# Small VectorE pieces handed out one a step, and a longer slack for the fill of two banks, in a gated mix of two attentions

## The chip, the core and the metric

The kernel runs on one core of one Trainium2 chip. The metric is the device time of one execution in microseconds (us), median of several runs. TensorE (PE) multiplies, VectorE (DVE) and ScalarE (ACT) read its results from PSUM, GpSimd (POOL) works in SBUF, SyncE (SP) only issues DMAs. Each engine works through its own queue in order and waits there for semaphores of the others.

## The reference

The output is a gated sum of two attentions over the same 2048 rows of 512 numbers, all in f32: branch A looks at eight earlier rows at distance 2, branch B is full attention of 32 heads on one shared key and value head.

```python
def _A_ref(x, wqkv, wo):          # H = 32, Dh = 16, W, dil = 8, 2
    ...
    logits = jnp.einsum("bhsd,bhswd->bhsw", q, kg) * scale
    logits = jnp.where(mask[None, None, :, :], logits, -1e9)
    attn = _softmax(logits, axis=-1)
    o = jnp.einsum("bhsw,bhswd->bhsd", attn, vg)
    return (lambda x, *d: x.transpose(*d))(o, 0, 2, 1, 3).reshape(B, S, D) @ wo

def _B_ref(x, wq, wk, wv, wo):    # H = 32, Dh = 16, one key and value head
    ...
    scores = jnp.einsum("bhqd,bkd->bhqk", q, k) * (Dh ** -0.5)
    p = _softmax(scores, axis=-1)
    o = jnp.einsum("bhqk,bkd->bhqd", p, v)
    return (lambda x, *d: x.transpose(*d))(o, 0, 2, 1, 3).reshape(B, S, H * Dh) @ wo

g = _sigmoid((x * gate_w).sum(-1, keepdims=True))
return g * _A_ref(...) + (1 - g) * _B_ref(...)
```

The inputs make the scores of branch B large, so that its softmax needs each row's maximum before the exponential.

## The kernel before, in words

**Units, steps, fills.** Branch B is cut into 32 units, each four heads by 512 queries. A unit takes 16 steps, one for each 128 keys, so the main loop (`for s in range(NS + 1)`, L737) has 512 steps. A step `s` multiplies keys by queries into two PSUM tiles of two banks each (`exp_pair`, L311: two matmuls at L316, then ScalarE's exponential at L318), and adds the weighted values of the step before into the one bank `po` (`weighted`, L323, matmuls at L326). At a unit's end VectorE transposes `po` (`finish_a`, L334, then `finish_b`), GpSimd divides and gates, and after every second unit VectorE transposes the result once more (`finish_c`, L354).

**Maxima.** Before a unit can start, the maximum of each of its 2048 query rows over all 2048 keys must be known. That takes 64 matmuls of 512 columns a unit ("fills", 2048 in all), each followed by a maximum on VectorE. `fill_pair` (L269) fills the two-bank tile `m2` (in the profile pm) with two of them and reduces both in one instruction (L274); `fill_one` (L278) fills the one-bank tile `m1` (in the profile ps) and reduces it (L285). Their matmuls are those of L253. When a unit's last fill is reduced, `filled` (L258) brings the unit's maxima together (two reduces at L264, a transpose at L266); `shift_a` (L289, ScalarE) and `shift_c` (L296, VectorE, L297) split them into two parts, and `shift_b` (L301) writes these by eight small DMAs into the rows of the stacked queries that subtract the maximum within the score matmul.

**The front.** Before the main loop, 78 lumps (14 of query projections, 64 of branch-A projections) are multiplied, with up to four fills after each (`front_fills`, L603, also into `eb[1]` and `po`).

**Branch A** runs on GpSimd in 16 groups. `run_pool` (L655) hands its pieces out when the planner's clock says that GpSimd will soon be free. Three steps of a group are on other engines, with a due time: the maximum (`a_max`, L395, VectorE), the exponential (`a_exp`, ScalarE) and the sum with its reciprocal (`a_sum`, L409, VectorE). Before they stand in a list `hooks`, and `run_pool` calls those that are due.

**Output.** Four times in the main loop `out_phase` (L512) multiplies four blocks of rows by the output weights, with fills between. `out_store` (L494) adds the two halves on GpSimd and stores them.

**What sets the order.** The schedule is written out by hand: the order in which the Python code issues instructions is the order of every queue. A planner decides it with three clocks (`clk` for PE, ACT, DVE) and fixed prices (L42). `after(engine, ready, price)` moves a clock on. `free[bank]` is when the planner believes a bank to be free again. `fill_ready(bank, slack)` (L559) issues a fill if the bank is free no later than `slack` after PE's clock; it then moves PE's clock to that time, so PE is expected to wait for so long. Otherwise the fill is left out of this step. Tasks with a due time are called by `run_tasks` (L598) at a step's end.

In a step of the main loop the order is: exponential pair, `fill_ready("m2")`, the other exponential pair, `fill_ready("m1")` if fills would otherwise not be done in time, `weighted`, `finish_a` at a unit's end, `run_tasks`, `run_pool`. An output phase starts when branch A is through and the fills are less than 1.6 units ahead.

Of the kernel before, what the change touches and what calls it, by code (L numbers as in the profile page):

```python
# [6 lines left out]
F32 = mybir.dt.float32  # L7
F32R = mybir.dt.float32r
AF = mybir.ActivationFunctionType
ALU = mybir.AluOpType  # L10
# [3 lines left out]
P = 128  # L14
# [23 lines left out]
NS = NU * NJ  # L38
NF = 2 * NU * 2 * 4 * 4


T_R, T_LAT, T_EXP, T_RED2, T_RED1, T_W, T_LUMP, T_Q = 0.23, 0.20, 0.92, 1.14, 0.61, 1.18, 2.53, 3.2  # L42


@with_exitstack
def gated_mix_kernel(ctx, tc, xt, wa, wk, wq, wo_a, wo_b, out):
# [33 lines left out]
    def after(eng, ready, dur):  # L80
        clk[eng] = max(clk[eng], ready) + dur
        return clk[eng]
# [168 lines left out]
    def max_mm(dst, v, pr, t, kc, odd):  # L251
        b = 64 * odd
        nc.tensor.matmul(dst, qst[v % NB][b:b + 62, pr, t * P:(t + 1) * P], kst[b:b + 62, kc * 512:(kc + 1) * 512], start=True, stop=True)  # L253

# [3 lines left out]
    def filled(v, n):  # L258
        left[v] -= n
        if not left[v]:  # L260
            ms = wp.tile([P, 2, 2, 8], F32, name="ms")
            m = mx.pop(v).rearrange("p b i t k -> p b (i t) k")
            for x in range(2):
                nc.vector.tensor_reduce(ms[:, :, x, :], m, AX.X, ALU.max)  # L264
            mt = wp.tile([P, 32], F32, name="mt")
            nc.vector.transpose(mt, ms.rearrange("p b x y -> p (b x y)"))  # L266
            tasks.append((after("dve", 0, 0.5) + 0.1, shift_a, (v, mt)))

    def fill_pair(dst, key):  # L269
        v, pr, t, kc = slots.pop(0)  # L270
        m = unit_tile(v)
        for odd in range(2):
            max_mm(dst[:, odd, :], v, pr, t, kc, odd)
        nc.vector.tensor_reduce(m[:, :, pr, t, kc], dst, AX.X, ALU.max)  # L274
        free[key] = after("dve", after("pe", 0, T_R) + T_LAT, T_RED2) + 0.08
        filled(v, 2)

    def fill_one(dst=m1, key="m1"):  # L278
# [5 lines left out]
        max_mm(dst, v, pr, t, kc, odd)  # L284
        nc.vector.tensor_reduce(m[:, odd, pr, t, kc:kc + 1], dst, AX.X, ALU.max)  # L285
        free[key] = after("dve", after("pe", 0, T_R) + T_LAT, T_RED1) + 0.08
# [9 lines left out]
    def shift_c(v, mt, th, ml):  # L296
        nc.vector.scalar_tensor_tensor(ml, mt, mk[:, 5:6], th.bitcast(F32), op0=ALU.mult, op1=ALU.add)  # L297
        after("dve", 0, 0.2)
        shift_b(v, ml)

# [193 lines left out]
    def out_store(j, n, k):  # L494
# [145 lines left out]

    hooks, pool, done = [], 0.0, set()
    QK, AV = 12500, 22500
# [12 lines left out]
    def run_pool():  # L655
        nonlocal pool
        now = clk["pe"] * 1e3
        while pieces and pool < now + 3000:
# [13 lines left out]
            elif kind == "qk1":  # L672
                a_scores(g, 1)
                pool += QK
                hooks.append((pool + 6000, a_max, g, "max"))
            elif kind == "sub":
                a_sub(g)
                pool += 800
                hooks.append((pool + 4000, a_exp, g, "exp"))
                hooks.append((pool + 6500, a_sum, g, "sum"))  # L680
            elif kind == "wo":
# [3 lines left out]
            else:  # L685
                a_values(g)
                pool += AV
        for h in sorted(hooks, key=lambda h: h[0]):
            if h[0] <= now:
                hooks.remove(h)  # L690
                h[1](h[2])
                done.add((h[3], h[2]))

# [43 lines left out]
    for s in range(NS + 1):  # L737
# [13 lines left out]
        lead = (NF - to_go()) / 64 - s / 16  # L751
        order = (0, "m2", 1, "m1") if s > 1 else (1, "m2", 0, "m1") if s else ()
        if not pieces and clk["pe"] * 1e3 > pool + 2000 and outs < NJ:
            n = C if outs < NJ - 4 else C - 1
            if s >= (16 * NHG * (outs // 4 + 1) + 4 if n == C else 16 * (NU - 2) + 4) and (lead < 1.6 or outs == 0 and s >= 400):
                out_phase(list(range(outs, outs + 4)), n)
                outs += 4
                order = (1, "m2", 0, "m1")
# [18 lines left out]
    assert not slots and not half and not hooks and not tasks and outs == NJ, (len(slots), len(hooks), len(tasks), outs)  # L777

# [59 lines left out]
```

## Time and profile before

| what | us |
|---|---|
| median of 3 runs (lowest, highest) | 1558.52 (1558.35, 1559.88) |
| the profiled execution's own time | 1558.82 |
| its span, first to last instruction | 1557.0 |
| first weighted matmul of the main loop starts | 315.13 |
| output phases, from the page's windows | 1010 to 1046, 1149 to 1184, 1285.5 to 1321, 1459.5 to 1490 |
| TensorE's mean granted clock | 0.998 |

In a row of the timeline stand start, length (both us), engine, line, operation, what it writes and reads, and how many instructions were merged; square brackets give the idle time before it and what ended it. In a row of groups stand line, engine, operation, tiles, shapes and count, then the total busy time and the mean of one in ns, then the idle time before. A row of a single source line gives its shortest, middle and longest duration, then its first and last start.

### The profile page before, as it was taken

The page shows a single profiled execution, that of the slowest core. Times are in us where ns is not written, and L with a number is a line of the kernel's source. Part 1 is how long each engine was busy: PE and PEld are TensorE (multiplying, and loading weights), DVE is VectorE, ACT ScalarE, POOL GpSimd, SP SyncE. Part 2 cuts the span into 40 slices and gives each one's busy share as a digit, 9 for nine tenths or more (in the row PEclk, how much of TensorE's full clock was granted, in tenths as well). Part 3 has the DMA queues.
Part 4 walks back from the last instruction along what each step waited for, and adds up shares of the span by engine and source line. Part 5 has one row for each costly group of instructions (what it writes and reads, how often), then busy time and mean ns, then how long its engine had stood idle before and what let it go on. Part 6 is the DMA issues. An engine that isn't in the chain of part 4 may idle for free.

```text
span 1557.0 us, 25703 instructions
## 1 busy us (share of the span) xinstructions
PE 1525.7 (98%) x10076; PEld 703.8 (45%) x10076; DVE 1335.8 (86%) x1667; ACT 1120.9 (72%) x1315; POOL 834.2 (54%) x1015
## 2 busy tenths in 40 slices
PE   8999999999999999999999999999999999999998
PEld 4677777733333333333333333363354336333532
DVE  6899999979888898888899889898898889888731
ACT  4223111189999899999989998939966993999676
POOL 7420897778987898889887885240031004000210
PEclk9999999999999999999999999999999999999999
DMA  7842312211011101211111010000000000000000
GB/s 240 261 141 90 120 62 91 99 59 41 21 49 49 56 19 50 65 47 34 50 49 56 20 48 12 22 28 12 12 19 21 12 2 29 2 2 1 2 1 27
DMA packets 42889, 78.61 MB, mean 50 GB/s; under 512 B 8544, under 2 KB 25024, under 8 KB 40720
## 3 DMA queue, kind: packets, MB, share of 16 engines
q1 hardware_dynamic: 20224, 35.56, 7.9%
q0 software_dynamic: 4640, 26.99, 5.0%
q10 hardware_dynamic: 17904, 14.42, 2.8%
q8 instruction: 79, 1.29, 0.3%
q14 instruction: 42, 0.34, 0.1%
HBM read 46.96 MB, written 29.45 MB: 49 GB/s over the span
## 4 chain that ended last, share of the span: by engine, by line
PE 82%; DVE 12%; ACT 4%; issue 1%; DMA 0%; DVEq 0%; POOL 0%; ACTq 0%
PE po L326 30%; PE pe L316 21%; PE pm L253 9%; PE ps L253 8%; DVE mx L274 7%; PE pe L529 5%; DVE mx L285 4%; ACT pexp L318 3%; PE pl L159 3%; PE pl L160 2%; PE pl L161 2%; PE pl L167 1%; PE pl L253 1%; DVE ml L297 0%; PE po L253 0%
## 5 line engine op out<-in xcount | busy, mean ns | idle before, releaser
L318 ACT ACTIVATE pexp<-pe 128x1024 f32<-128x1024 f32 x1022 | 989.2, 1022 | 105.2 <-PE pe L316 100.4
L274 DVE TENSOR_REDUCE mx<-pm 128x2 f32<-128x1024 f32 x610 | 743.9, 1219 | 144.3 <-PE pm L253 140.9
L326 PE MATMUL po<-pexp,vst 128*32 128x512 f32 x4088 | 545.3, 605 | 0.7 <-ACT pexp L318 0.6
L316 PE MATMUL pe<-qst,kst 64*128 64x512 f32 x2044 | 467.0, 452 | 11.1 <-ACT pexp L318 5.8
L316 PEld LDWEIGHTS pe<-qst,kst 64*128 64x128 f32 x2044 | 191.1, 184 | 518.4 <-ACT pexp L318 506.2
L285 DVE TENSOR_REDUCE mx<-ps 128x1 f32<-128x512 f32 x597 | 405.5, 679 | 0.0
L253 PE MATMUL pm<-kst,qst 62*128 62x512 f32 x1230 | 262.6, 417 | 0.8 <-DVE mx L274 0.2
L253 PE MATMUL ps<-kst,qst 62*128 62x512 f32 x597 | 242.6, 406 | 0.4
L381 POOL TENSOR_TENSOR pr<-aext 128x512 f32<-128x512 f32 x128 | 163.9, 1302 | 57.1 <-DMA aext<-ad 57.0
L326 PEld LDWEIGHTS po<-pexp,vst 128*32 128x32 f32 x4088 | 80.4, 108 | 176.4 <-issue 163.3
L206 ACT ACTIVATE stage<-pl 128x384 f32<-128x384 f32 x64 | 31.5, 492 | 165.3 <-PE pl L161 162.8
L426 POOL TENSOR_TENSOR oa<-oa,av 128x512 f32<-128x512 f32 x112 | 143.5, 1281 | 8.8
L346 POOL TENSOR_TENSOR rl<-rl,gate_t 128x16 f32<-128x16 f32 x31 | 6.8, 220 | 242.6 <-DVE rl L342 242.6
L253 PEld LDWEIGHTS pm<-kst,qst 62*128 62x128 f32 x1230 | 117.4, 186 | 41.4 <-DVE mx L274 17.2
L253 PEld LDWEIGHTS ps<-kst,qst 62*128 62x128 f32 x597 | 111.1, 186 | 30.4 <-DVE mx L285 22.3
L424 POOL TENSOR_TENSOR av<-aext,lg 128x512 f32<-128x512 f32 x112 | 118.9, 1061 | 7.5
L305 POOL DMA_DIRECT2D qst<-ml x48 | 27.3, 573 | 134.6 <-DVE ml L297 130.8
L159 PE MATMUL pl<-wah,xh 128*128 128x384 f32 (+1 forms) x256 | 93.7, 366 | 0.4 <-ACT stage L206 0.4
L274 DVE TENSOR_REDUCE mx<-pl 128x2 f32<-128x1024 f32 x75 | 91.1, 1215 | 0.0
L160 PE MATMUL pl<-wal,xh 128*128 128x384 f32 (+1 forms) x256 | 87.1, 340 | 0.0
L161 PE MATMUL pl<-wah,xl 128*128 128x384 f32 (+1 forms) x256 | 86.9, 339 | 0.0
L529 PE MATMUL pe<-woh,turned 64*128 64x512 f32 x496 | 84.3, 400 | 0.1
(124 smaller groups left out, 1204.4 us busy)
## 6 DMA issues: line engine op xcount, KB each, us to landing
aext<-ad POOLq DMA_DIRECT2D x16, 1440.0 KB, 6.2
qst<-qd SPq DMA_DIRECT2D x64, 192.0 KB
ad<-stage ACTq DMA_DIRECT2D x32, 384.0 KB
qd<-qhi SPq DMA_DIRECT2D x32, 256.0 KB
xraw<-xt SPq DMA_DIRECT2D x16, 256.0 KB
qd<-qlo SPq DMA_DIRECT2D x16, 256.0 KB
qst<-ml SPq DMA_DIRECT2D x208, 2.0 KB
out<-two SPq DMA_DIRECT2D x12, 256.0 KB
```

Of the source, the lines that this page charges most:

```text
L159: mms.append(lambda c=c: nc.tensor.matmul(out_ap, ah(c), bh(c), start=(c == 0), stop=False))
L160: mms.append(lambda c=c: nc.tensor.matmul(out_ap, ah(c), bl(c), start=False, stop=False))
L253: nc.tensor.matmul(dst, qst[v % NB][b:b + 62, pr, t * P:(t + 1) * P], kst[b:b + 62, kc * 512:(kc + 1) * 512], start=True, stop=True)
L274: nc.vector.tensor_reduce(m[:, :, pr, t, kc], dst, AX.X, ALU.max)
L285: nc.vector.tensor_reduce(m[:, odd, pr, t, kc:kc + 1], dst, AX.X, ALU.max)
L316: nc.tensor.matmul(bank[:, odd, :], kst[b:b + 64, kt * P:(kt + 1) * P], qst[u % NB][b:b + 64, pr, :], start=True, stop=True)
L318: nc.scalar.activation(e, bank, AF.Exp, scale=SCALE)
L326: nc.tensor.matmul(po[32 * i:32 * i + 32, :], vst[:, kt, :], pexp[s, i // 2][:, i % 2, :], start=(kt == 0), stop=(kt == NJ - 1))
L381: nc.gpsimd.tensor_mul(pr[:, k], q, e[:, o:o + NJ, AC:2 * AC])
L424: nc.gpsimd.tensor_mul(av, e[:, o:o + NJ, 2 * AC:].rearrange("p j (h d) -> p j h d", d=DH), lg[:, w].unsqueeze(3).to_broadcast([P, NJ, AG, ...
L426: nc.gpsimd.tensor_add(ao, ao, av)
L529: nc.tensor.matmul(eb[x % 2][:, b, :], st[h], mv[h], start=first, stop=last)
```

## The change

It has these parts:

- **Small pieces.** The closing of a unit's maxima becomes a task of its own (`close`); so does `shift_b`, which ran within `shift_c`. `a_max`, `a_exp` and `a_sum` go from the list `hooks` into the same list of tasks. In the main loop `run_tasks(True)` issues at most one small VectorE task (`close`, `shift_c`, `finish_c`, `a_max`, `a_sum`) a step, and none while VectorE's clock is over `BEHIND` = 0.9 ahead of PE's.
- **Slack.** `fill_ready` gets 0.9 for the pair (0.15 before) and 0.35 for the single (0.15 before). Steps 0 and 512 get fills too.
- **Halves.** Each maximum is taken over 256 columns, not 512: the reduces write twice as many values, the tile of maxima is twice as wide and has two buffers for three, and the closing reduces read 128 values for 64.
- **Prices.** The weighted matmuls 1.18 to 1.21, the closing 0.5 to 0.66, the shift 0.2 to 0.45, `finish_b` 0.8 to 0.96.
- **Queues.** The stores of three output phases go from SP's queue to GpSimd's.

```diff
+BEHIND = 0.9
+M2S = 0.9
+M1S = 0.35
-T_R, T_LAT, T_EXP, T_RED2, T_RED1, T_W, T_LUMP, T_Q = 0.23, 0.20, 0.92, 1.14, 0.61, 1.18, 2.53, 3.2
+T_R, T_LAT, T_EXP, T_RED2, T_RED1, T_W, T_LUMP, T_Q = 0.23, 0.20, 0.92, 1.14, 0.61, 1.21, 2.53, 3.2
...
-            mx[v] = wp.tile([P, 2, 2, 4, 4], F32, name="mx", bufs=3)
+            mx[v] = wp.tile([P, 2, 2, 4, 8], F32, name="mx", bufs=2)
...
         if not left[v]:
-            ms = wp.tile([P, 2, 2, 8], F32, name="ms")
-            m = mx.pop(v).rearrange("p b i t k -> p b (i t) k")
-            for x in range(2):
-                nc.vector.tensor_reduce(ms[:, :, x, :], m, AX.X, ALU.max)
-            mt = wp.tile([P, 32], F32, name="mt")
-            nc.vector.transpose(mt, ms.rearrange("p b x y -> p (b x y)"))
-            tasks.append((after("dve", 0, 0.5) + 0.1, shift_a, (v, mt)))
+            tasks.append((clk["dve"], close, (v, mx.pop(v).rearrange("p b i t k -> p b (i t) k"))))
+
+    def close(v, m):
+        ms = wp.tile([P, 2, 2, 8], F32, name="ms")
+        for x in range(2):
+            nc.vector.tensor_reduce(ms[:, :, x, :], m, AX.X, ALU.max)
+        mt = wp.tile([P, 32], F32, name="mt")
+        nc.vector.transpose(mt, ms.rearrange("p b x y -> p (b x y)"))
+        tasks.append((after("dve", clk["pe"], 0.66) + 0.1, shift_a, (v, mt)))
...
-        nc.vector.tensor_reduce(m[:, :, pr, t, kc], dst, AX.X, ALU.max)
+        nc.vector.tensor_reduce(m[:, :, pr, t, 2 * kc:2 * kc + 2], dst.rearrange("p o (h n) -> p o h n", h=2), AX.X, ALU.max)
...
-        nc.vector.tensor_reduce(m[:, odd, pr, t, kc:kc + 1], dst, AX.X, ALU.max)
+        nc.vector.tensor_reduce(m[:, odd, pr, t, 2 * kc:2 * kc + 2], dst.rearrange("p (h n) -> p h n", h=2), AX.X, ALU.max)
...
-        after("dve", 0, 0.2)
-        shift_b(v, ml)
+        tasks.append((after("dve", clk["pe"], 0.45) + 0.1, shift_b, (v, ml)))
...
-        at = after("dve", clk["pe"] + T_LAT, 0.8)
+        at = after("dve", clk["pe"] + T_LAT, 0.96)
...
-            nc.sync.dma_start(out[0].rearrange("(p j) d -> p j d", j=NJ)[:, j, :], two[:, 0])
+            nc.gpsimd.dma_start(out[0].rearrange("(p j) d -> p j d", j=NJ)[:, j, :], two[:, 0])
...
-        while n < most and slots and fillable():
+        while n < most and fillable():
...
-    def run_tasks():
+    def run_tasks(spread=False):
+
         for task in [t for t in tasks if t[0] <= clk["pe"]]:
+            small = task[1] in (close, shift_c, finish_c, a_max, a_sum)
+            if small and spread == 2 or spread and small and clk["dve"] > clk["pe"] + BEHIND:
+                continue
             tasks.remove(task)
             task[1](*task[2])
+            if small:
+                spread = spread and 2
+            if len(task) > 3:
+                done.add(task[3])
...
-                hooks.append((pool + 6000, a_max, g, "max"))
+                tasks.append(((pool + 6000) / 1e3, a_max, (g,), ("max", g)))
...
-                hooks.append((pool + 4000, a_exp, g, "exp"))
-                hooks.append((pool + 6500, a_sum, g, "sum"))
+                tasks.append(((pool + 4000) / 1e3, a_exp, (g,), ("exp", g)))
+                tasks.append(((pool + 6500) / 1e3, a_sum, (g,), ("sum", g)))
...
-        order = (0, "m2", 1, "m1") if s > 1 else (1, "m2", 0, "m1") if s else ()
+        order = (0, 1) if s > 1 else (1, 0) if s else ()
...
-        for which in order:
-            if which == "m2":
-                fill_ready("m2", 0.15)
-            elif which == "m1":
-                ahead = 2 * (16 * (NU - 2) - 8 - s) + 11 * (NJ - 4 - outs)
-                if ahead < to_go() - NF // NU or s >= 16 * (NU - 2) - 8 and ahead + 64 < to_go():
-                    fill_ready("m1", 0.15)
-            elif s < NS:
-                exp_pair(s, which)
+        ahead = 2 * (16 * (NU - 2) - 8 - s) + 11 * (NJ - 4 - outs)
+        more = ahead < to_go() - NF // NU or s >= 16 * (NU - 2) - 8 and ahead + 64 < to_go()
+        if order and s < NS:
+            exp_pair(s, order[0])
+            fill_ready("m2", M2S)
+            exp_pair(s, order[1])
+        else:
+            fill_ready("m2", M2S)
+        if more:
+            fill_ready("m1", M1S)
...
-        run_tasks()
+        run_tasks(True)
```

More of the change, by code (lines that the diff above doesn't have):

```diff
@@ L246, in unit_tile, with max_mm @@
         if v not in mx:
-            mx[v] = wp.tile([P, 2, 2, 4, 4], F32, name="mx", bufs=3)
+            mx[v] = wp.tile([P, 2, 2, 4, 8], F32, name="mx", bufs=2)
             left[v] = NF // NU
         return mx[v]
-    def max_mm(dst, v, pr, t, kc, odd):
-        b = 64 * odd
-        nc.tensor.matmul(dst, qst[v % NB][b:b + 62, pr, t * P:(t + 1) * P], kst[b:b + 62, kc * 512:(kc + 1) * 512], start=True, stop=True)
+    def max_mm(dst, v, pr, t, kc, odd, k=0, n=512):
+        b, k = 64 * odd, 512 * kc + k
+        nc.tensor.matmul(dst, qst[v % NB][b:b + 62, pr, t * P:(t + 1) * P], kst[b:b + 62, k:k + n], start=True, stop=True)
     def to_go():
@@ L639, in gated_mix_kernel @@
     load_wa(0)
-    hooks, pool, done = [], 0.0, set()
+    pool, done = 0.0, set()
     QK, AV = 12500, 22500
@@ L687, in run_pool @@
                 pool += AV
[L688 to L692, printed above, removed]
     lumps += [("q", m) for m in range(2, 4 * NQB)]
@@ L757, in gated_mix_kernel @@
                 outs += 4
[L758 removed]
+                order = (1, 0)
         elif short > 0 and steps < 2:
             pause(short)
[L762 to L770 removed]
+        ahead = 2 * (16 * (NU - 2) - 8 - s) + 11 * (NJ - 4 - outs)
[8 more added lines that the diff above has]
+            fill_ready("m1", M1S)
         if s:
@@ L774, in gated_mix_kernel @@
                 finish_a(u - 1, nc.gpsimd)
-        run_tasks()
+        run_tasks(True)
         run_pool()
-    assert not slots and not half and not hooks and not tasks and outs == NJ, (len(slots), len(hooks), len(tasks), outs)
+    assert not slots and not half and not tasks and outs == NJ, (len(slots), len(tasks), outs)
     for x in range(8):
```

## The prediction

> A *pair* below is a fill through the two-bank tile pm (two matmuls, one reduce), a *single* one through ps (one matmul, one reduce); a *step* is one turn of the main loop.
>
> **What bounds the kernel now.** I read the page's busy shares and its chain of waits first, then the windows by stretch.
>
> ```profile
> PE 1525.7 (98%) x10076; PEld 703.8 (45%) x10076; DVE 1335.8 (86%) x1667; ACT 1120.9 (72%) x1315; POOL 834.2 (54%) x1015
> PE 82%; DVE 12%; ACT 4%; issue 1%; DMA 0%; DVEq 0%; POOL 0%; ACTq 0%
> ```
>
> Of the windows (columns: stretch, length, then busy time and count of PE, PEld, DVE, ACT, POOL):
>
> ```profile
> 200.00:316.00 116.00, 114.82 (x594) 87.23 (x592) 115.25 (x147) 21.80 (x42) 97.21 (x123) 1.00 0.26 84
> 316.00:1010.00 694.00, 690.95 (x4761) 247.93 (x4757) 613.72 (x768) 628.03 (x675) 554.50 (x684) 1.00 0.13 41
> ```
>
> In the last 116 us of the front VectorE is busy for 115.25: there it sets the time. In the main loop nobody is full on average, so one quiet step decides what sets it. The timeline of PE, of ScalarE and of VectorE:
>
> ```profile
> 702.57 1.07 PE L326 MATMUL po<-pexp,vst 128*32 128x512 f32 x8
> 703.57 0.50 PE L316 MATMUL pe<-qst,kst 64*128 64x512 f32 x2
> 703.91 0.40 PE L253 MATMUL pm<-kst,qst 62*128 62x512 f32 x2
> 704.14 0.40 PE L316 MATMUL pe<-qst,kst 64*128 64x512 f32 x2
> 704.37 0.40 PE L253 MATMUL ps<-kst,qst 62*128 62x512 f32 x1
> 704.70 1.07 PE L326 MATMUL po<-pexp,vst 128*32 128x512 f32 x8
> ```
>
> ```profile
> 704.17 1.94 ACT L318 ACTIVATE pexp<-pe 128x1024 f32<-128x1024 f32 x2 [0.18 <-PE pe L316]
> ```
>
> ```profile
> 703.36 0.68 DVE L285 TENSOR_REDUCE mx<-ps 128x1 f32<-128x512 f32 x1
> 704.35 1.23 DVE L274 TENSOR_REDUCE mx<-pm 128x2 f32<-128x1024 f32 x1 [0.30 <-PE pm L253]
> ```
>
> The step is 704.70 - 702.57 = 2.13 us, PE without a hole; ScalarE waits 0.18 and VectorE 0.30 in it. The single's reduce ends at 703.36 + 0.68 = 704.04 and its bank is written again at 704.37, 0.33 later. So VectorE can take a small piece of up to 0.30 + 0.33 = 0.63 us between two steps before PE waits for a bank. What a single costs, and how far the loop is from quiet, comes from windows of the weighted matmuls alone (eight records a step) and of the fills:
>
> ```profile
> 321.40:1010.20 688.80, 338.81 (x2544) 50.03 (x2544) 1.00 0.13 42
> 1431.40:1459.50 28.10, 14.92 (x112) 2.20 (x112) 1.00 0.01 1
> L253 PE MATMUL ps<-kst,qst 62*128 62x512 f32 x312 | 126.3, 405 | 0.0
> ```
>
> Steps with pairs alone (1431 to 1459) take 28.10/14 = 2.01 us, ScalarE's pace; so a single costs 2.13 - 2.01 = 0.12. While branch A runs (321 to 1010) 318 steps take 688.80/318 = 2.166, which is 318 x 0.036 = 11.4 us over quiet ones. They hold 312 singles: six steps were left without a fill.
>
> **The change part by part.** The order within a step (exp, pair, exp, single, weighted) stays; so do the number of fills and of VectorE's pieces. What can move is when fills and pieces are issued.
>
> *No step skipped (slack 0.15 to 0.9 and 0.35).* A skipped step:
>
> ```profile
> 664.00 1.06 PE L326 MATMUL po<-pexp,vst 128*32 128x512 f32 x8
> 665.87 1.06 PE L326 MATMUL po<-pexp,vst 128*32 128x512 f32 x8
> 668.26 1.06 PE L326 MATMUL po<-pexp,vst 128*32 128x512 f32 x8
> ```
>
> and VectorE's pieces in it:
>
> ```profile
> 663.24 0.71 DVE L336 STREAM_TRANSPOSE tt<-po 128x512 f32<-128x512 f32 x1
> 664.15 0.55 DVE L411 TENSOR_REDUCE asum<-lg 128x32 f32<-128x256 f32 x1
> 664.73 0.35 DVE L412 RECIPROCAL asum<-asum 128x32 f32<-128x32 f32 x1
> ```
>
> The output's transpose and a branch-A sum met in one step, the planner saw VectorE behind and left out both fills. Two steps take 668.26 - 664.00 = 4.26 = 2 x 2.13, so the skip itself loses nothing but its three halves, which the planner makes good by three singles elsewhere. Six skips are 18 singles: **-2.2 us** (0 if the banks still come too late for 0.9).
>
> *What these six steps cost when they are filled.* The pieces that the skip absorbed now push PE. The same two pieces one step apart, fills kept:
>
> ```profile
> 562.21 1.07 PE L326 MATMUL po<-pexp,vst 128*32 128x512 f32 x8
> 564.80 1.07 PE L326 MATMUL po<-pexp,vst 128*32 128x512 f32 x8
> ```
>
> ```profile
> 561.64 0.62 DVE L411 TENSOR_REDUCE asum<-lg 128x32 f32<-128x256 f32 x1
> ```
>
> The step is 564.80 - 562.21 = 2.59, 0.46 over quiet. Behind a waiting pair in PE's queue stand the second exp's matmuls, and ScalarE waits for those. A meeting costs between 0 (pieces three steps apart) and about 0.6 (in successive steps, each a little late); I take 0.3, the middle: six make **+1.8** (0 to +3.6).
>
> *Pieces spread.* Of the 11.4 us over quiet, spreading reaches only what comes from several pieces in one step, or from a unit's end handed out between the two reduces. Two steps' starts, then the first and the last of four unit ends that fell in the middle of a step, between the pair's and the single's reduce:
>
> ```profile
> 644.61 1.06 PE L326 MATMUL po<-pexp,vst 128*32 128x512 f32 x8
> 646.95 1.06 PE L326 MATMUL po<-pexp,vst 128*32 128x512 f32 x8
> 645.19 0.34 DVE L264 TENSOR_REDUCE ms<-mx 128x16 f32<-128x64 f32 x2
> 838.19 0.34 DVE L264 TENSOR_REDUCE ms<-mx 128x16 f32<-128x64 f32 x2
> ```
>
> and a branch-A sum with nothing beside it:
>
> ```profile
> 612.13 1.06 PE L326 MATMUL po<-pexp,vst 128*32 128x512 f32 x8
> 614.53 1.07 PE L326 MATMUL po<-pexp,vst 128*32 128x512 f32 x8
> ```
>
> Such an end costs 2.34 - 2.13 = 0.21, which goes when it waits for the step's end; four make 0.8. The lone sum, 2.40 - 2.13 = 0.27, is one piece by itself: an order cannot make it shorter. I take **-1.5**, twice the unit ends (bounds 0 and -4.0, a third of the 11.4, if the lone sums too fall where VectorE has room).
>
> One piece is out of the planner's hands:
>
> ```profile
> L297 DVE SCALAR_TENSOR_TENSOR ml<-mt,mk,mh x32: 231/244/1360, 114.1 to 1494.9; 128x32 fp32r<-128x32 f32 x32
> 794.96 1.29 DVE L297 SCALAR_TENSOR_TENSOR ml<-mt,mk,mh 128x32 fp32r<-128x32 f32 x1
> 794.91 2.55 POOL L381 TENSOR_TENSOR pr<-aext 128x512 f32<-128x512 f32 x2
> ```
>
> The 0.24 us shift took 1.29 while GpSimd ran, ending (796.25) about when GpSimd's first of two ended (794.91 + 2.55/2 = 796.19). The new code counts 0.45 for it; what GpSimd holds it up is in no term, since GpSimd's work is unchanged. The Trainium skill, "SBUF — State Buffer", section "Who interferes with whom", states that a VectorE instruction with two SBUF inputs and a GpSimd instruction that reads SBUF exclude each other for a whole instruction. By that rule handing the shift out later cannot shorten it, which speaks against a larger gain; were the length mere queueing, it would fall with the spread and the term above would go towards its -4.0. The trace agrees with the rule in the two ends above.
>
> *The pieces themselves.* The maxima now come in halves, so each reduce writes twice as many values, and the two closing reduces read 128 values instead of 64.
>
> ```profile
> L264 DVE TENSOR_REDUCE ms<-mx 128x16 f32<-128x64 f32 x14 | 2.4, 214 | 0.2
> L153 DVE TENSOR_REDUCE mk<-ident 128x1 f32<-128x64 f32 x1 | 0.2, 207 | 0.0
> L411 DVE TENSOR_REDUCE asum<-lg 128x32 f32<-128x256 f32 x3 | 1.8, 597 | 0.0
> L274 DVE TENSOR_REDUCE mx<-pl 128x2 f32<-128x1024 f32 x75 | 91.1, 1215 | 0.0
> L285 DVE TENSOR_REDUCE mx<-ps 128x1 f32<-128x512 f32 x75 | 50.9, 679 | 0.0
> ```
>
> Sixteen results instead of one from 64 values: 214 - 207 = 7 ns, 0.5 ns a result. The strided sum bounds it above: (597 - 207 - 192 x 1.05)/31 = 6 ns. 64 values more cost 64 x (1215 - 679)/512 = 67 ns a reduce, 0.13 us a unit. In the VectorE-bound front that goes straight to the time: five of its seven unit ends (14 closing reduces) there, +0.7, and 116/3.46 = 34 lumps (two pairs and two singles: 2 x 1.215 + 2 x 0.679 less overlap) of six more results, 0.1 (at 6 ns, 1.2; nearest row taken). In the loop the other 25 unit ends grow by 0.13 each, part of it inside the 0.63 that costs nothing: 0 to 0.13 each, I take 0.03, so 0.7. Together **+1.5** (0.8 to 5.2).
>
> *Edits at nothing.* The stores to GpSimd's queue: an engine idle for 46% of the span has room for 12 more issues, and SP's queue then holds no store in front of the shifts; were GpSimd full, the stores would trail the adds and only the last could show. The shift's DMAs go out a task, so some steps of 2 us, later. The transpose row shows what covers them at the tightest place:
>
> ```profile
> L336 DVE STREAM_TRANSPOSE tt<-po x31: 694/706/718, 351.6 to 1514.5; 128x512 f32<-128x512 f32 x31
> ```
>
> the last unit begins at 1514.5, and the last shift (above) ran at 1494.9, 20 us ahead; without that lead PE stops at the unit's start. The weighted price 1.18 to 1.21 makes the planner's step 2.13, the measured one, and with it hands out branch A's pieces a per cent sooner; GpSimd's idle 140 of 694 us covers that.
>
> Sum: -2.2 + 1.8 - 1.5 + 1.5 = **-0.4 us** against the profiled execution's 1558.82 us (span 1557.0), so 1558.4; the median of the runs shown is 0.3 lower, which gives **1558.1**.
>
> **The rivals.** *Faster*: the planner's step now matches the measured one, so branch A's pieces, which met the output's transpose at the same place in the unit again and again, drift past it. Then the six filled steps cost 0.1 each and spreading gets its -4.0: -2.2 + 0.6 - 4.0 + 1.5 = -4.1, 1554.4. For it: the two meetings quoted, at 561.64 and 664.15, are 102.5 us or 48 steps apart, three whole units. Against: lone sums and GpSimd-bound shifts stay.
>
> *Slower*: the wait in PE's queue takes the place of the skip. Place: the pair's matmuls in the branch-A stretch. VectorE gains back 0.30 us a step and the planner believes 2.13 - 1.14 - 0.61 = 0.38; it prices a sum at 0.6 where its two instructions take 0.55 + 0.35 = 0.9. Pieces follow in successive steps as long as it believes VectorE under 0.9 behind, and each finds the last one's backlog. It decides from the point where two pieces of over 0.6 us come within two steps. One such meeting for each branch-A group in the stretch (16 less the three sums of the front, x3 above, is 13) at 0.46, with nothing won by spreading: -2.2 + 6.0 + 1.5 = +5.3, 1563.8. For it: 564.80. Against: VectorE is idle for 80 of 694 us.
>
> *It does not do what it says*: the planner's clock seldom sees VectorE late (six times in 318 steps), so nearly the same order comes out and only the longer pieces count: +1.5, 1560.0, inside the first case.
>
> **How the numbers follow.** This kernel's runs differ by 0.1%, so I count under 0.2%, 3.1 us, as no change. No change holds 0.36 (my sum 0.28, the idle edit 0.08), faster 0.32, slower 0.32: each rival rests on one kind of row, and they face each other evenly. The likeliest is 1558.1, its own range 1555.4 to 1561.6. The rivals lie 4 and 5 us off; with the bounds of the reduce's price and of the spread a range of **1552.5 to 1565.0** leaves out about 2 in 10.
>
> **What would show it.** Right: in the profile after, the stretch with branch A has a single in every step and about 20 fewer singles before the end; its mean step stays between 2.15 and 2.18; the pair's reduce (128x4) keeps 1.22 us; closing reduces take 0.28. Wrong: matmuls of pm waiting long for mx in PE's queue and ScalarE's idle time behind pe growing (slower), or a mean step near 2.145 (faster); a reduce at 1.25 or more would lengthen the front by over 1 us.

## The result, and the profile after

The changed kernel takes **1566.0 us** (median of 5 runs, 1563.82 to 1568.61) beside 1559.5 (1558.35 to 1561.45, 5 runs) for the kernel before: a ratio of 1.0042, 95% interval 1.0028 to 1.0057. It is slower by 6.5 us and lies 1 us beyond the upper end of the predicted range. The profiled execution took 1566.0, with a span of 1564.2 against 1557.0.

The page of the kernel after: busy shares, the chain of waits, the costliest reduces.

```profile
PE 1524.4 (97%) x10076; PEld 704.4 (45%) x10076; DVE 1338.3 (86%) x1665; ACT 1121.3 (72%) x1315; POOL 840.2 (54%) x1027
PE 73%; DVE 13%; POOL 8%; ACT 4%; DMA 1%; issue 1%; DVEq 0%; ACTq 0%; POOLq 0%
L279 DVE TENSOR_REDUCE mx<-pm 128x4 f32<-128x1024 f32 x613 | 745.7, 1216 | 148.1 <-PE pm L256 145.3
L290 DVE TENSOR_REDUCE mx<-ps 128x2 f32<-128x512 f32 x596 | 404.8, 679 | 0.0
```

No engine works longer than before in a way that could explain 7 us: PE is busy for 1.3 us less. What is new is in the second line: GpSimd, absent from the chain before, holds 8% of it. The chain led back to an engine that is idle for 46% of the span, because something on the path waited for it once.

Where the time went is seen from the weighted matmuls alone (windows, columns stretch, length, PE, PEld, clock, DMA share, GB/s), from the end of step 1 to that of step 319, as the prediction showed it for before:

```profile
319.40:1016.70 697.30, 339.64 (x2544) 50.08 (x2544) 1.00 0.14 41
```

The same 318 steps (2544/8) take 697.3 us instead of 688.8: **+8.5**, a mean step of 2.193. What lies ahead of them is 2.0 shorter (319.4 against 321.4), what lies behind 0.7 longer (1564.2 - 1016.7 = 547.5 against 1557.0 - 1010.2 = 546.8). So the loss is in the branch-A stretch, and more than all of it.

About two thirds of it is one place. The timeline of the kernel after (start, duration, engine, operation; in brackets the idle time before it and what ended that):

```profile
501.24 1.06 PE L330 MATMUL po<-pexp,vst 128*32 128x512 f32 x8
505.79 0.80 PE L320 MATMUL pe<-qst,kst 64*128 64x512 f32 x2 [3.48 <-ACT pexp L322]
506.38 0.63 PE L256 MATMUL pm<-kst,qst 62*128 62x512 f32 x2
507.85 1.93 PE L330 MATMUL po<-pexp,vst 128*32 128x512 f32 x8
511.46 1.07 PE L330 MATMUL po<-pexp,vst 128*32 128x512 f32 x8
...
504.41 0.42 ACT L410 ACTIVATE lg<-lg 128x256 f32<-128x256 f32 x1 [3.90 <-POOL lg L406]
...
503.65 0.72 POOL L406 TENSOR_TENSOR lg<-lg,amx 128x256 f32<-128x256 f32 x1
```

Branch A's exponential (L410) stood at the head of ScalarE's queue when GpSimd had not yet begun the difference that it reads (L406). ScalarE waited 3.90 us for it, with branch B's exponentials queued behind; PE, which needs them, waited 3.48. Then a second loss: the matmul pairs that take 0.40 to 0.50 elsewhere take 0.63 to 0.80, and eight weighted ones 1.93 instead of 1.06. The windows there (columns stretch, length, PE, PEld, DVE, ACT, POOL, granted clock, DMA share, GB/s):

```profile
502.30:504.30 2.00, 0.01 (x1) 0.00 (x0) 1.03 (x4) 0.00 (x0) 1.84 (x5) 0.99 0.00 0
504.30:511.10 6.80, 5.31 (x21) 2.36 (x22) 2.80 (x5) 4.87 (x7) 6.49 (x9) 0.50 0.01 2
511.00:515.00 4.00, 4.00 (x30) 1.30 (x28) 4.00 (x5) 3.49 (x4) 3.76 (x5) 0.99 0.01 2
```

PE's last matmul before the pause ends at 502.30. For 2.00 us the granted clock stays at 0.99; from 504.30, still within the pause, it is 0.50 for 6.80 us. From one weighted group's end to the next two, the steps take 507.85 + 1.93 - 501.24 - 1.06 = 7.48 and 511.46 + 1.07 - 507.85 - 1.93 = 2.75 instead of 2.13 each: 6.0 us for a wait of 3.90. (A second wait of this kind, 1.19 us at 403, makes another 1.3.) The Trainium skill, "TensorE: Matmul & The Clock Gate", section "What's actually happening", says that PE drops to half its clock after an idle window of about 3.4 us. The trace agrees on the half, 0.50, but not on the time: here it came 2.0 us into the pause, and the measurement decides (the last section has shorter pauses).

In the kernel before the same exponential never waited. Lines of ScalarE in the window 330 to 1015, first before:

```profile
L406 ACT ACTIVATE lg<-lg 128x256 f32<-128x256 f32 x13 | 5.4, 419 | 0.0
```

then after:

```profile
L410 ACT ACTIVATE lg<-lg 128x256 f32<-128x256 f32 x13 | 5.4, 419 | 5.1 <-POOL lg L406 5.1
```

And how near it was, in the timeline of before, for the same group:

```profile
503.78 0.73 POOL L402 TENSOR_TENSOR lg<-lg,amx 128x256 f32<-128x256 f32 x1
...
506.71 0.42 ACT L406 ACTIVATE lg<-lg 128x256 f32<-128x256 f32 x1
```

GpSimd's difference ends at 504.51 there and at 504.37 after: GpSimd is as fast and at the same place. The exponential began 2.20 us later in before. That margin was the planner's guess, and it was about one step. In the groups at about 354, 403, 453 and 504 it was 2.72, 2.88, 4.13 and 2.20 us in before, and 1.64 and then three times 0.03 in after (0.03 means that the exponential began as soon as the difference was there).

### The profile page after: what moved, and what is told of

The parts are those of the page before. It is cut to its first block, busy times and chain, and to the rows that moved or that the text cites. A ratio compares the mean times of both kernels' runs of the same rounds, so it can differ in the third digit from the quotient of the medians.

```text
span 1564.2 us, 25703 instructions
## 1 busy us (share of the span) xinstructions
PE 1524.4 (97%) x10076; PEld 704.4 (45%) x10076; DVE 1338.3 (86%) x1665; ACT 1121.3 (72%) x1315; POOL 840.2 (54%) x1027
## 4 chain that ended last, share of the span: by engine, by line
PE 73%; DVE 13%; POOL 8%; ACT 4%; DMA 1%; issue 1%; DVEq 0%; ACTq 0%; POOLq 0%
PE po L330 26%; PE pe L320 18%; PE pm L256 8%; DVE mx L279 7%; PE ps L256 7%; PE pe L533 5%; DVE mx L290 4%; ACT pexp L322 3%; PE pl L162 2%; PE pl L164 2%; PE pl L163 2%; POOL oa L430 2%; POOL pr L385 2%; POOL tr L390 2%; POOL av L428 1%
## 5 line engine op out<-in xcount | busy, mean ns | idle before, releaser
L279 DVE TENSOR_REDUCE mx<-pm 128x4 f32<-128x1024 f32 x613 | 745.7, 1216 | 148.1 <-PE pm L256 145.3
L290 DVE TENSOR_REDUCE mx<-ps 128x2 f32<-128x512 f32 x596 | 404.8, 679 | 0.0
L279 DVE TENSOR_REDUCE mx<-pl 128x4 f32<-128x1024 f32 x74 | 89.6, 1211 | 0.0
L390 POOL TENSOR_TENSOR tr<-pr 128x512 f32<-128x512 f32 x64 | 81.5, 1274 | 5.0
```

The costliest lines, as they stand in the source:

```text
L279: nc.vector.tensor_reduce(m[:, :, pr, t, 2 * kc:2 * kc + 2], dst.rearrange("p o (h n) -> p o h n", h=2), AX.X, ALU.max)
L290: nc.vector.tensor_reduce(m[:, odd, pr, t, 2 * kc:2 * kc + 2], dst.rearrange("p (h n) -> p h n", h=2), AX.X, ALU.max)
```

## The experiments

**First question: is it the clocks that place branch A's exponential?** The planner hands it out when PE's clock passes GpSimd's plus 4.0 us. The theory: raising the weighted price to 1.21 moved PE's clock against GpSimd's, so ScalarE reached the exponential too early. The rival: the wide slack makes PE wait where pieces follow each other. The expectations call the first the price theory or the clock theory, the rival the queue theory.

*The price alone taken out of the change, and put alone into the kernel before.*

```diff
-T_R, ..., T_W, ... = 0.23, 0.20, 0.92, 1.14, 0.61, 1.21, 2.53, 3.2    # after
+T_R, ..., T_W, ... = 0.23, 0.20, 0.92, 1.14, 0.61, 1.18, 2.53, 3.2
```

> The changed kernel with the weighted matmuls priced 1.18 again, all else as changed. Price theory: the planner's clock of PE runs 1.4% slower against the chip again, so branch A's exponential is handed to ScalarE later in the program, after GpSimd has subtracted the maximum; ScalarE's waits for lg in the main loop (1.19 and 3.90 us in the profile after, around 402 and 504 us) fall below 1 us in all, and the time falls by 4 to 6 us, to about 1560 to 1562 us. Queue theory (PE waits for banks because of the longer slack and of pieces in successive steps): the waits for banks stay, 1565 to 1567 us.

Measured 1562.42 (11 runs), ratio 1.0019 (1.001 to 1.0028): rather more than half of the loss is gone. In its profile the exponential does not wait within 330 to 1015. That execution took 1559.19, 3 us below its median, so it shows only a part of the rest (the table below).

> The kernel before with the one price 1.18 changed to 1.21. Price theory: ScalarE now waits for GpSimd in front of branch A's exponential, 3 us or more in the main loop, and the time rises by 3 to 6 us over before, to 1562 to 1565 us. Queue theory: nothing that makes PE wait is changed, 1558 to 1561 us.

Measured 1562.57, ratio 1.0028 (1.0018 to 1.0037): the one number costs the kernel before 4 us. Its lines in the same window:

```profile
L406 ACT ACTIVATE lg<-lg 128x256 f32<-128x256 f32 x13 | 5.5, 420 | 3.7 <-POOL lg L402 3.7
```

*The change kept, the exponential moved.* Once by its due time, once by GpSimd's price for the products, which moves everything that is due behind them.

```diff
-                tasks.append(((pool + 4000) / 1e3, a_exp, (g,), ("exp", g)))
-                tasks.append(((pool + 6500) / 1e3, a_sum, (g,), ("sum", g)))
+                tasks.append(((pool + 7500) / 1e3, a_exp, (g,), ("exp", g)))    # e3
+                tasks.append(((pool + 9500) / 1e3, a_sum, (g,), ("sum", g)))
...
-    QK, AV = 12500, 22500
+    QK, AV = 13300, 22500                                                       # e9
```

> The changed kernel with the due time of branch A's exponential 3.5 us later and that of its sum 3 us later (planner's time). Price theory: ScalarE's wait of 3.90 us falls to under 1 and the one of 1.19 to none, the time falls by 4 to 6 us to 1560 to 1562 us, though the price is still 1.21. Queue theory: the pieces of VectorE are as many and as close, 1565 to 1567 us.

> The changed kernel with the planner's price of each half of branch A's scores on GpSimd at 13.3 in place of 12.5 us, all due times as changed. Clock theory: a group then takes 50.4 us in the planner's GpSimd clock, as in the trace (first product of group 5 to that of group 6: 440.8 - 390.3 = 50.5 us), so its pieces no longer run ahead of GpSimd, ScalarE's waits for lg in the main loop fall under 1 us, and the time falls by 4 to 8 us, to 1558 to 1562 us, without touching a due time. If the waits come from something else, 1565 to 1567 us.

Measured 1558.22, ratio 0.9993 (0.9985 to 1.0002), and 1557.34, ratio 0.9998 (0.9989 to 1.0007): each is back at the time of before. But they don't get there in the same way. The lines of the window, first of the one with the later due time, then of the one with the other GpSimd price:

```profile
L410 ACT ACTIVATE lg<-lg 128x256 f32<-128x256 f32 x13 | 5.4, 419 | 3.4 <-POOL lg L406 3.4
L410 ACT ACTIVATE lg<-lg 128x256 f32<-128x256 f32 x13 | 5.4, 419 | 0.0
```

The stages of the profiled executions, from the ends of the weighted matmuls (all in us; the last column is a part of the rest, from the first to the last start of that phase's matmuls with the output weights):

| | to the end of step 1 | steps 2 to 319 | the rest | third output phase |
|---|---|---|---|---|
| before | 321.4 | 688.8 | 546.8 | 31.0 |
| after | 319.4 | 697.3 | 547.5 | 33.0 |
| price 1.18 (e1) | 319.0 | 691.0 | 547.4 | 33.0 |
| later due times (e3) | 316.0 | 694.9 | 545.6 | 30.4 |
| GpSimd's price (e9) | 319.0 | 691.7 | 545.5 | 30.5 |

The last column comes from lines like these, of before, after and e9:

```profile
L529 PE MATMUL pe<-woh,turned x128: 383/390/495, 1286.5 to 1317.5; 64*128 64x512 f32 x128
L533 PE MATMUL pe<-woh,turned x128: 383/392/500, 1325.4 to 1358.4; 64*128 64x512 f32 x128
L533 PE MATMUL pe<-woh,turned x128: 383/393/501, 1312.9 to 1343.4; 64*128 64x512 f32 x128
```

Without a wait for the difference the 318 steps take 5.6 to 6.3 us less than after (e9, e1). In e3 the waits are only shorter: 3.4 us in all, the longest 1.84 instead of 3.90, against an expectation of under 1; its steps gain 2.4, and more of its gain lies ahead of them, which was not explained. A second loss is in the last column: the third output phase takes 2.0 us longer in after and in e1, and not in e3 and e9. So these two also win back something that is not the exponential's wait. What it is, the end of the next section shows; no run takes it out alone.

*The exponential sooner still*: due 2.0 us after GpSimd's clock instead of 4.0.

> The changed kernel with branch A's exponential 2 us sooner: the opposite dose. Clock theory: ScalarE's waits for lg in the main loop grow from 5.1 us to 10 us or more, over more groups; each wait over about 1.6 us also halves PE's granted clock for some us after it, so the time rises by 5 to 15 us, to 1571 to 1581 us. If the exponential's place did not matter: 1564 to 1568 us.

Measured 1564.58, ratio 1.0054 (1.0042 to 1.0067). It wasn't clearly worse, and the expectation missed. The wait in the loop was shorter and in another group:

```profile
402.28 0.42 ACT L410 ACTIVATE lg<-lg 128x256 f32<-128x256 f32 x1 [2.37 <-POOL lg L406]
...
403.66 0.50 PE L320 MATMUL pe<-qst,kst 64*128 64x512 f32 x2 [1.96 <-ACT pexp L322]
405.60 1.94 PE L330 MATMUL po<-pexp,vst 128*32 128x512 f32 x8
```

At 505 the exponential began 0.94 us after the difference. Tasks are handed out at steps' ends, so an exponential moves by whole steps of 2.13 and shifts the pieces behind it. This may be why the loss doesn't grow in proportion to the due time. Why this group and not that one, the runs don't tell.

**Second question: what do the parts do by themselves?** Each is put alone into the kernel before, or taken alone out of the one after. The maxima by halves (e7), the wide slacks (e5), and the spreading: the order of hand-outs of the kernel after with weighted price 1.18, both slacks 0.15, whole maxima, finish price 0.8, stores on SP and no fills at step 0 (e6).

```diff
-                fill_ready("m2", 0.15)        # e5
+                fill_ready("m2", 0.9)
...
-                    fill_ready("m1", 0.15)
+                    fill_ready("m1", 0.35)
```

> The kernel before with the maxima taken over 256 columns in place of 512 (reduces that write twice as many values, closing reduces over 128 values, two buffers of maxima). Both theories: 0.13 us more a unit end, 0 to 1.5 us in all, 1558.5 to 1560 us. Over 1561 us would mean that the reduces themselves take longer.

Measured 1560.69, ratio 1.0012 (1.0003 to 1.0021): 2 us, a little more than the 1.5 that was expected at most.

> The kernel before with the two slacks of the change alone (0.9 and 0.35 for 0.15 each). Clock theory (the planner's clock of PE, pushed on by every wait it allows, calls branch A's exponential before GpSimd has subtracted, and ScalarE waits): the six steps without a fill go and about 9 to 18 singles are saved, 1 to 2 us; the planner's waits put its clock forward by a few us, and a wait of ScalarE of 0 to 2 us comes back; 1556 to 1560 us. Queue theory (PE's waits for banks are what costs): PE waits longer for mx, 1561 to 1564 us.

Measured 1564.06, ratio 1.0027 (1.0018 to 1.0036): the rival's cost is real in this kernel. No wait for GpSimd's difference is in its loop, and it loses about two thirds of what the change loses (1.0042).

> The spreading alone: tasks for the closing, the shift's DMAs and branch A's pieces, at most one small piece of VectorE a step, prices of the closing and the shift as changed; the slacks, the weighted price, the halves and the stores' queue as before. Clock theory: the clock is hardly touched, so ScalarE does not wait longer than 1 us in the main loop, and the time stays within 2 us of before, 1557 to 1560 us. Queue theory: the pieces follow in successive steps and the time rises by 3 us or more.

Measured 1563.96, ratio 1.0034 (1.0022 to 1.0047), a miss: with the price at 1.18 the exponential waited all the same. The line of the window 330 to 1015:

```profile
L410 ACT ACTIVATE lg<-lg 128x256 f32<-128x256 f32 x13 | 5.4, 418 | 3.4 <-POOL lg L406 3.4
```

Here the hooks have become tasks and small pieces wait for one another, so the order is another one too: the price is one way of losing the margin and not the only one.

*The change without spreading* (all due pieces at once):

```diff
-        run_tasks(True)
+        run_tasks()
```

> The changed kernel, but in the main loop all due pieces of VectorE are handed out in one step, as before the change. Price theory: ScalarE's waits for lg stay within 1 us of those after, 1564 to 1568 us. Queue theory: pieces no longer follow in successive steps, so PE's waits for mx fall and the time drops by 3 us or more, to 1563 us or less.

Measured 1569.56, ratio 1.0065 (1.0052 to 1.0078): worse than with it, and beyond what either theory gave. Its exponential waits 3.4 us in the window, and in two output phases PE stands for 1.65 us behind a shift.

**Third question: with the exponential out of the way, what are slack and spreading worth?** All of these have exponential and sum due later (the edit of e3). e13 is the kernel before with that alone, e14 adds the wide slacks (e5), e15 is the spreading alone (e6). e8 is the kernel after with price 1.18, e11 that with whole maxima, e17 is e8 without spreading.

> The kernel before with its branch-A exp due 3.5 us and its sum 3.0 us later on the planner's clock. If a late exp helps only where ScalarE would have waited for GpSimd's difference (none in the loop of the kernel before), no change: 1557.5 to 1560. If the gain of the two kernels that beat the one before is the exp's place alone and nothing of the change, then 1554 to 1556.

> The kernel before with the wide slacks, and exp and sum due later. If the wide slack has a price of its own (the wait in PE's queue where pieces follow in successive steps), it stays at 1562 to 1565; if only the places of exp and sum made that run slow, 1556 to 1560.

> The spreading alone, and exp and sum due later. If its loss was the two waits of ScalarE for GpSimd's difference and the slow clock behind them, 1555 to 1560; if spreading has a price of its own, 1562 to 1566.

> The changed kernel with the weighted price 1.18 and branch A's exponential 3.5 us and its sum 3 us later. Clock theory: both put the exponential later, so no wait of ScalarE for lg is left in the main loop; what stays is the gain of fewer singles against longer closings, 1555 to 1558 us, below before. Queue theory: 1562 us or more, as with the weighted price alone.

> The version with the weighted price 1.18 and the later exponential (1554.96 us in its run), with the maxima over 512 columns again. Measured for the halves alone on the kernel before: +0.12%. Clock theory: the saving is the 0.13 us a unit end, 0.5 to 2.5 us, 1552.5 to 1554.5 us. If the halves cost nothing here, 1554 to 1556 us.

> The version of 1554.96 (weighted price 1.18, exp and sum later) with all due small pieces handed out at once again. If one piece a step is what keeps the wide slack from costing what it costs alone (6 us), 1559 to 1565, with steps over 3 us where a finish and a shift meet; if the spreading does nothing for the time, 1554 to 1557.

| all with a later exponential | slack | spreading | us | ratio to before (95%) |
|---|---|---|---|---|
| e13, kernel before | small | no | 1557.98 | 1.0002 (0.9993 to 1.0011) |
| e15, spreading alone | small | yes | 1556.93 | 0.9998 (0.9988 to 1.0008) |
| e14, slack alone | wide | no | 1564.70 | 1.0040 (1.0028 to 1.0052) |
| e17, kernel after without spreading | wide | no | 1560.94 | 1.0013 (1.0004 to 1.0023) |
| e8, kernel after | wide | yes | **1554.96** | **0.9975 (0.9964 to 0.9986)** |
| e11, the same with whole maxima | wide | yes | **1554.70** | **0.9979 (0.9971 to 0.9988)** |

The later exponential gives the kernel before nothing, as its profile said: it had no wait to lose. It does give e6 back its loss (1.0034 to 0.9998). The wide slack alone costs 6.7 (e14 against e13); spreading alone gains at most a microsecond; but taking the spreading out of e8 costs 6.0. So **the two parts belong together** (e8 has the change's other prices and queue as well), and with both the change beats the kernel before by 0.2%, once the exponential is late enough. The halves make no difference there (e8, e11).

What the wide slack does without spreading is seen in e14's timeline:

```profile
455.36 0.71 DVE L336 STREAM_TRANSPOSE tt<-po 128x512 f32<-128x512 f32 x1
456.50 1.30 DVE L297 SCALAR_TENSOR_TENSOR ml<-mt,mk,mh 128x32 fp32r<-128x32 f32 x1
...
456.12 1.07 PE L326 MATMUL po<-pexp,vst 128*32 128x512 f32 x8
459.00 0.50 PE L253 MATMUL pm<-kst,qst 62*128 62x512 f32 x2 [1.38 <-DVE mx L274]
460.01 1.66 PE L326 MATMUL po<-pexp,vst 128*32 128x512 f32 x8
463.61 1.11 PE L326 MATMUL po<-pexp,vst 128*32 128x512 f32 x8
...
459.78 1.02 ACT L318 ACTIVATE pexp<-pe 128x1024 f32<-128x1024 f32 x1 [1.04 <-PE pe L316]
```

The output's transpose, its reciprocal and a shift meet between two steps. The shift, priced 0.2, takes 1.30 beside GpSimd. The next pair's bank is 1.38 us late, the second exponential's matmuls are queued behind that pair, ScalarE waits 1.04, and the clock falls (the weighted matmuls take 1.66). From 456.12 to 463.61 two steps take 7.49 instead of 4.26: 3.2 us for one meeting. Whether leaving the fills out there would have cost less was not run; in e13, with the small slack, this shift falls two steps behind the transpose. In e17, without spreading, the same three pieces meet, and a step takes 983.06 - 979.57 = 3.49:

```profile
979.57 1.07 PE L330 MATMUL po<-pexp,vst 128*32 128x512 f32 x8
982.04 0.50 PE L256 MATMUL pm<-kst,qst 62*128 62x512 f32 x2 [0.98 <-DVE mx L279]
983.06 1.07 PE L330 MATMUL po<-pexp,vst 128*32 128x512 f32 x8
```

In e8 the shift comes two steps behind the transpose:

```profile
975.39 0.71 DVE L340 STREAM_TRANSPOSE tt<-po 128x512 f32<-128x512 f32 x1
...
979.80 0.74 DVE L302 SCALAR_TENSOR_TENSOR ml<-mt,mk,mh 128x32 fp32r<-128x32 f32 x1
```

*Small slacks in the whole change.* e8 with both slacks 0.15, then with the finish priced 0.8 again as well.

```diff
-M2S = 0.9
-M1S = 0.35
+M2S = 0.15                                     # e12, e16
+M1S = 0.15
...
-        at = after("dve", clk["pe"] + T_LAT, 0.96)
+        at = after("dve", clk["pe"] + T_LAT, 0.8)   # e16
```

> The version with the weighted price 1.18 and the later exponential, with both slacks back at 0.15. Clock theory (the gain of that version is the fewer singles that the slack brings): steps without a fill return, six to nine singles come back, 1556 to 1559 us. Queue theory (the slack costs more in waits for banks than it saves, as the slack alone on the kernel before did with +0.27%): faster than with the slack, 1550 to 1554 us.

> The slow run with small slacks (1594.8), with the finish priced 0.8 again in place of 0.96. If the larger price is what makes the planner leave out both fills at each unit's second step, 1555 to 1562 and no catching up of 12 to 22 us; if small slacks starve the fills as soon as pieces are spread, over 1580.

e12 took 1594.82, ratio 1.0243 (1.0229 to 1.0257), by far the widest miss. In its timeline a unit's second step has no fill at all, and much later the missing maxima are made up at once:

```profile
348.95 1.07 PE L330 MATMUL po<-pexp,vst 128*32 128x512 f32 x8
349.95 0.95 PE L320 MATMUL pe<-qst,kst 64*128 64x512 f32 x4
350.82 1.06 PE L330 MATMUL po<-pexp,vst 128*32 128x512 f32 x8
...
997.26 1.94 ACT L322 ACTIVATE pexp<-pe 128x1024 f32<-128x1024 f32 x2 [9.15 <-PE pe L320]
```

The finish at a unit's end, believed to take 0.96, puts the bank further off than 0.15 allows; fills are left out there until a unit's maxima are due and the planner pauses for them, with ScalarE idle for 9.15 us. e16 took 1563.91, ratio 1.0032 (1.0021 to 1.0044), above the 1562 that was expected, but 31 us less than e12: the finish's price starved the fills. Small slack and the larger price don't go together; the slack that was widened is what makes the larger price harmless. e16 remains slow; two shifts like the following are part of it (its timeline; the other lies at 1304.73). Behind step 319 it takes 553.4 us, where e15 takes 547.9:

```profile
1165.31 2.65 DVE L302 SCALAR_TENSOR_TENSOR ml<-mt,mk,mh 128x32 fp32r<-128x32 f32 x1
...
1165.39 1.30 POOL L469 TENSOR_TENSOR turned<-ob,turned 128x512 fp32r<-128x512 f32 x1
1166.64 1.27 POOL L483 TENSOR_TENSOR turned<-own,turned 128x512 fp32r<-128x512 f32 x1
```

## Why the prediction was wrong, point by point

**The step that failed** is in "Edits at nothing": "The weighted price 1.18 to 1.21 makes the planner's step 2.13, the measured one, and with it hands out branch A's pieces a per cent sooner; GpSimd's idle 140 of 694 us covers that." The sentence saw the effect and looked at the wrong engine. GpSimd's idle time covers nothing: the piece that came sooner is an instruction on **ScalarE**, in order, with the loop's exponentials behind it, and what mattered was the distance between it and GpSimd's difference, 2.20 us in before's timeline. The trace was there to be read. The edit costs the kernel before 4 us by itself (e2); taken out of the change it gives back rather more than half of the loss (e1); and with GpSimd's price mended no wait for the difference is left in the loop (e9). How a correct price does harm is in GpSimd's own rows of before, for four groups:

```profile
L402 POOL TENSOR_TENSOR lg<-lg,amx x5: 729/735/737, 352.3 to 553.5; 128x256 f32<-128x256 f32 x5
L381 POOL TENSOR_TENSOR pr<-aext 128x512 f32<-128x512 f32 x32 | 41.0, 1300 | 21.0 <-DMA aext<-ad 21.0
```

A group takes (553.5 - 352.3)/4 = 50.3 us, 21.0/4 = 5.3 of them spent waiting for its load; the planner counts 2 x 12.5 + 0.8 + 22.5 + 0.5 = 48.8 (0.5 for the load), 3% too little. PE's step was counted 2.10 (2.13 less the 0.03 of the edit) where 2.166 were measured, 3% too little. Two errors of the same size cancelled; the change mended one. That e9, which mends the other (2 x 13.3 + 23.8 = 50.4), takes the waits out, and that the margins shown above shrink in after and not in before, speaks for this reading; the planner's clocks themselves were not recorded.

*What these six steps cost when they are filled* (+1.8, at most 3.6): wrong in kind and far too small. The wide slack alone costs 5 to 7 us (e5, e14), with the singles that it saves already counted, and the single meeting quoted costs 3.2 where 0.6 was the bound: three pieces, one of them held up by GpSimd, met in a step's end, and the clock fell behind the wait. *Pieces spread* (-1.5, bounds 0 and -4.0): spreading was priced in a kernel with small slack, where it is indeed worth nothing much (e15); with the wide slack it is worth 6.0 (e8, e17). The two terms were right in sign and each too small by several us, and they hang on each other; that their sum, +0.3, is not far from 6.7 - 6.0 is luck.

*No step skipped* (-2.2): the skips went. Lines of the kernel after, 319.4 to 1016.7:

```profile
L256 PE MATMUL ps<-kst,qst 62*128 62x512 f32 x318 | 129.6, 407 | 0.0
```

All 318 steps have their single. But of the 18 halves only 9 came off the later singles (201 after that stretch instead of 210), 9 x 0.12 = 1.1 us; the others took away pairs. *The pieces themselves* (+1.5): the pair's reduce kept 1.216 and the single's 0.679, the closing reduces grew as said, in the lines of VectorE by form:

```profile
L269 DVE TENSOR_REDUCE ms<-mx 128x16 f32<-128x128 f32 x64 | 15.0, 275 | 0.1
```

and the whole cost lies between nothing (e11 against e8) and 2 us (e7). The stretch ahead of the steps got shorter by 2.0 rather than longer by 0.8. About half of it is step 1: in before's profiled execution the granted clock was 0.50 there (318.0 to 321.4), in after's 1.00, so that part need not be the change's doing.

The slower rival gave 1563.8, near the time, but by luck: its mechanism is hardly in the changed kernel, where matmuls of pm wait 2.2 us for VectorE in the whole page. What happens without spreading (e14, e17) is near to it, but there the pieces meet in one step and not in successive ones. Of the signs named, "a single in every step", the reduce at 1.22 and the closing at 0.28 held; "a mean step between 2.15 and 2.18" and "about 20 fewer singles" did not.

Outside branch A the shift was met as well, in the third output phase of the kernel after:

```profile
1345.32 2.54 DVE L302 SCALAR_TENSOR_TENSOR ml<-mt,mk,mh 128x32 fp32r<-128x32 f32 x1
...
1348.51 0.49 PE L256 MATMUL ps<-kst,qst 62*128 62x512 f32 x1 [1.61 <-DVE mx L290]
```

PE waits 1.61 us for VectorE behind a 2.54 us shift. This is the third output phase that takes 2.0 us longer than before. The prediction left it in no term "since GpSimd's work is unchanged"; its work is, but not what it meets. So this is a second, smaller step that failed, read from the profiles alone: it is there in after and e1, and gone in e3, e8 and e9.

## What to carry to other kernels

In a hand-written order that several clocks steer, a price is not better for being nearer to the measurement: two errors may cancel, so mend them together, or check each instruction whose due time mixes two clocks for its margin in the trace (start of the reader less end of the writer) before one of the clocks is touched. A piece handed to another engine's queue must be costed on the engine whose queue it stands in, not on the one that makes its data. And parts of a change that look independent are not: a bank awaited longer needs its small pieces spread.

## What the runs showed of the hardware

PE's clock fell after shorter pauses than the first section's. In e14 PE stood still for 1.38 us, up to 459.00, and the granted clock (window columns as above) was then 0.55:

```profile
460.00:463.60 3.60, 3.60 (x16) 1.31 (x15) 2.09 (x3) 1.90 (x3) 3.44 (x5) 0.55 0.02 3
```

Pauses of one length went both ways. Behind a shift in the third output phase PE stood for 1.65 us in e4 and in e1; first the lines of e4, then those of e1:

```profile
1351.06 0.79 PE L256 MATMUL ps<-kst,qst 62*128 62x512 f32 x1 [1.65 <-DVE mx L290]
1351.00:1354.40 3.40, 3.34 (x16) 2.69 (x18) 2.10 (x4) 0.00 (x0) 2.01 (x4) 0.51 0.05 5
...
1341.64 0.49 PE L256 MATMUL ps<-kst,qst 62*128 62x512 f32 x1 [1.65 <-DVE mx L290]
1341.60:1345.00 3.40, 3.36 (x28) 2.42 (x30) 3.37 (x4) 0.41 (x1) 1.98 (x4) 1.00 0.05 5
```

So the pause's length alone does not decide, and no bound of about 1.6 us, as the expectation of e10 has it, holds. The Trainium skill, "TensorE: Matmul & The Clock Gate", section "Why this matters for your kernels", warns of pauses over about 3 us; here half the clock followed a pause of 1.38 once, and the measurement decides. So in this loop a wait of little over a microsecond could cost more than its length.

The other surprise is a 0.24 us VectorE instruction that took 2.54 (after) and 2.65 (e16): as long as two GpSimd instructions in a row (1165.39 to 1167.91, the shift ending at 1167.96). In the prediction's row it had waited for one. Here it ended only behind the second as well, though by the trace it had begun before that one. The Trainium skill, "SBUF — State Buffer", section "Who interferes with whom", says that of two such instructions the one that is issued first holds the ports for its whole length. For the first of the two the trace can't tell (it begins at 1165.39, the shift at 1165.31); the second (1166.64) went ahead of the shift all the same.
